# A block-sparse kernel whose expert numbers reach TensorE's registers in nine pieces instead of two loads

## Chip, cores and metric

One core of one Trainium2 chip runs the whole program. The metric is the device time of an execution in microseconds. TensorE (PE in the profile) multiplies matrices and has a stream for weight loads and register work of its own (PEld, PEldq); VectorE is DVE, ScalarE is ACT, GpSimd is POOL, SyncE is SP, which mostly issues DMAs.

## What is computed

Three parts run one behind the other in a single launch. A chunked linear attention over 4 x 8 x 768 x 32 values gives 3072 tokens of 256 channels. A first, dense "MoE" follows, and then a second one, with eight experts, of which each token takes the one with the largest gate:

```python
h = x @ w_in                       # 3072 x 256 -> 2048
x = (h * np.cos(h)) @ w_out        # 2048 -> 256
...
expert_idx = np.argmax(x @ w_gate, axis=1)
gate_w = probs[np.arange(N), expert_idx]
# each expert keeps its first `capacity` (768) tokens
h = np.maximum(np.einsum('ecd,edf->ecf', disp, w1), 0.0)   # 256 -> 1024
y = np.einsum('ecf,efd->ecd', h, w2)                       # 1024 -> 256
out[i] = gate_w[i] * y[expert_idx[i], pos[i]]
```

Which tokens go to which expert is known only when the kernel runs.

## The kernel before, in words

The tokens of the second MoE are sorted by expert into blocks of 128, each of one expert. There can be up to 31 blocks; 29 are always run, two more only behind a test at the end. The blocks come in two parts: 12 "early" blocks, from the tokens that have left the first MoE by then, and up to 19 "late" ones. Each part has a table, `eblk[0]` and `eblk[1]`, in which position n holds the expert number of its nth block. It is built by VectorE (L1141 to L1143).

A block's work is cut into two jobs, one for each half of the 1024 hidden channels; j counts the 58 jobs in order. The first 16 jobs are the first halves of blocks 0 to 15; the second halves of these come last. A job has these steps:

- `b_mm1` (L1603): six products of 128 x 512 into `hp`. The weights of the block's expert are picked by a register: `w[:, bass.ds(ev[i], 1), ...]`, so TensorE must hold block i's expert number in a register by then.
- `b_relu` (L1609, ScalarE) and `b_low` (L1613, VectorE) write the high and the low half-precision part of the result, `hr`.
- `b_turn`: for jobs 0 to 15 eight transposes on TensorE (L1630) that ScalarE copies to `ht` (L1639), for later jobs one transpose by DMA from SP's queue (L1634).
- `b_mm2` (L1650): twelve products of 128 x 256 into `yp`, with a register again. `b_out` (L1662 on ScalarE, L1664 on VectorE) scales and adds them, and `b_scat` (L1669, GpSimd) scatters a finished block.

`b_gather` and `b_xt` fetch a block's tokens (L1535) and transpose them by DMA (L1552). Beside the jobs run the units that prepare the second half's weights, `mk3` with `w2_units`: a pair of tiles `wst` is loaded from SP's queue (L1223, 512 KB a tile), ScalarE sums the squares of each (L1231), TensorE adds these over the partitions with two tiny products into `pn` (L1235), VectorE makes scales of that (L1240 to L1243), and the tiles are written as a high and a low part (L1250, L1252, L1256).

The registers are filled by `experts(k)`, once for each part of the blocks:

```python
regs = [nc.tensor.alloc_register(f"e{i}") for i in range(lo, hi)]
nc.tensor.reg_load(regs, eblk[k][0:1, 0:hi - lo])      # L1592
for i, r in zip(range(lo, hi), regs):
    ev[i] = nc.tensor.snap(r, min_val=0, max_val=E - 1)  # L1594
```

The load is one instruction on TensorE's sequencer (TENSOR_LOAD in the profile), and the register operations behind it show as FUSED_REGOPS. TensorE's loads, register operations and products are issued from one stream, in order.

The order of all this is written out by hand. The table `PLACE` gives every step a number; `put(name, fn, ...)` takes the next number of its name, and the steps are emitted by rising number, on all engines. `ex0` and `ex1` are the names under which `experts(0)` and `experts(1)` stand.

Of the kernel before, what the change touches and what calls it, by code (L numbers as in the profile page):

```python
# [95 lines left out]
    'con': [100],  # L96
    'cp': [188, 327, 352, 483, 628, 726, 836, 965, 1093, 1224],
    'css': [1523, 1570, 1609, 1639, 1670, 1687, 1709, 1747],
# [5 lines left out]
    'dfi': [206, 212, 232, 236, 345, 285, 302, 328],  # L104
    'et': [1404],
# [6 lines left out]
    'ex0': [1472],  # L112
    'ex1': [1658],
# [9 lines left out]
    'id': [1513],  # L123
    'in0': [1502],
    'in1': [1667],
    'iv0': [1499],
    'iv1': [1756, 1757, 1762],
    'lt': [1592],
    'lte': [1643],
    'lts': [1607],  # L130
    'ltt': [1623],
# [130 lines left out]
    'rev': [402, 403, 658, 661, 889, 895, 1113, 1123, 1328, 1329, 1517, 1520],  # L262
    'rex': [1245, 1405, 1576],
    'rg1': [565, 783, 1016, 1232, 1359, 1567],
    'rg2': [625, 846, 1083, 1295, 1421, 1578],
    'rh0': [479, 689, 957, 1192, 1370, 1535],
    'rh2': [502, 775, 984, 1280, 1385, 1557],
    'rl0': [497, 745, 967, 1195, 1384, 1545],
    'rl2': [648, 847, 1039, 1299, 1397, 1581],
# [11 lines left out]
    'rst': [662, 923, 1122, 1300, 1434, 1599],  # L281
    'rx0': [406, 675, 901, 1127, 1332, 1521],
    'rx1': [432, 670, 912, 1132, 1330, 1522],
    'rx2': [471, 712, 953, 1167, 1352, 1540],
    'rx3': [450, 706, 917, 1139, 1334, 1537],
# [20 lines left out]
    'uh': [1325, 1371, 1435, 1506],  # L306
    'ul': [1344, 1351, 1408, 1409, 1476, 1463, 1515, 1530],
    'un': [1287, 1360, 1411, 1461],
    'used': [1863],
# [25 lines left out]
def fused_kernel(ctx: ExitStack, tc: tile.TileContext, I, out: bass.AP):  # L335
    nc = tc.nc
# [42 lines left out]
    NE = 12  # L379
    LOS = ((0, NE), (NE, NB))  # L380
    gat = [base.tile([P, 20], I32, name=f"gat{k}") for k in range(2)]
    scat = [base.tile([P, 20], I32, name=f"scat{k}") for k in range(2)]
    eblk = [base.tile([P, 20], I32, name=f"eblk{k}") for k in range(2)]
# [894 lines left out]
    def put(name, fn, *a):  # L1278
        k = seen.get(name, 0)
        seen[name] = k + 1  # L1280
        work.append((PLACE[name][k], len(work), fn, a))
# [113 lines left out]
    for it in range(NIT):  # L1395
        t, f = divmod(it, NF)
# [192 lines left out]
    def experts(k):  # L1589
        lo, hi = LOS[k]  # L1590
        regs = [nc.tensor.alloc_register(f"e{i}") for i in range(lo, hi)]
        nc.tensor.reg_load(regs, eblk[k][0:1, 0:hi - lo])  # L1592
        for i, r in zip(range(lo, hi), regs):
            ev[i] = nc.tensor.snap(r, min_val=0, max_val=E - 1)  # L1594
# [105 lines left out]
    put('ete', t_expert, 0)  # L1700
    put('ett', t_token, 0)
    put('ex0', experts, 0)
    put('lt', late_tables)
    put('lts', t_sum, 1)
    put('lte', t_expert, 1)
    put('ltt', t_token, 1)
    put('ex1', experts, 1)
    put('iv0', b_iv, 0)
    put('in0', b_inv, 0, 0)
# [24 lines left out]
    used = []  # L1734
# [77 lines left out]
```

## Time and profile before

| | us |
|---|---|
| median of three executions (568.5 to 569.3) | 568.72 |
| the profiled execution, its own time | 568.56 |
| its span, first to last instruction | 566.8 |
| TensorE busy | 528.7 (93%) |
| VectorE busy | 415.7 (73%) |
| ScalarE busy | 379.2 (67%) |
| GpSimd busy | 355.6 (63%) |

The mean granted clock of TensorE over the span is 0.984. The shares are means over stages with different limits, so they say little of one place; the profiled execution's time and its span differ by what lies before the first and behind the last instruction.

### The profile page before, as it was taken

The page shows a single profiled execution, that of the slowest core. Times are in us where ns is not written, and L with a number is a line of the kernel's source. Part 1 is how long each engine was busy: PE and PEld are TensorE (multiplying, and loading weights), DVE is VectorE, ACT ScalarE, POOL GpSimd, SP SyncE. Part 2 cuts the span into 40 slices and gives each one's busy share as a digit, 9 for nine tenths or more (in the row PEclk, how much of TensorE's full clock was granted, in tenths as well). Part 3 has the DMA queues.
Part 4 walks back from the last instruction along what each step waited for, and adds up shares of the span by engine and source line. Part 5 has one row for each costly group of instructions (what it writes and reads, how often), then busy time and mean ns, then how long its engine had stood idle before and what let it go on. Part 6 is the DMA issues. An engine that isn't in the chain of part 4 may idle for free.

```text
span 566.8 us, 10500 instructions
## 1 busy us (share of the span) xinstructions
PE 528.7 (93%) x3188; PEld 387.9 (68%) x3188; DVE 415.7 (73%) x877; ACT 379.2 (67%) x691; POOL 355.6 (63%) x422
## 2 busy tenths in 40 slices
PE   8778999999999999999999998899589999998993
PEld 7455666877878778887888686665357666665672
DVE  6999985669977987688788999989957632332441
ACT  5448998887788688868887887788388633323210
POOL 5775374878668869876955673887546454312454
PEclk9999999999999999999999998999789999999998
DMA  6898533666264365263522331576587688767882
GB/s 227 276 318 323 191 116 128 186 246 220 94 222 132 99 201 177 82 201 116 166 58 76 85 102 38 144 185 174 139 198 204 113 160 162 157 118 131 152 164 63
DMA packets 110645, 89.91 MB, mean 159 GB/s; under 512 B 64542, under 2 KB 99424, under 8 KB 110592
## 3 DMA queue, kind: packets, MB, share of 16 engines
q1 hardware_dynamic: 107808, 82.26, 52.5%
q0 software_dynamic: 2784, 6.97, 4.8%
q8 instruction: 30, 0.49, 0.4%
q14 instruction: 23, 0.19, 0.1%
HBM read 59.50 MB, written 15.54 MB: 132 GB/s over the span
## 4 chain that ended last, share of the span: by engine, by line
PE 45%; DVE 25%; ACT 11%; DMA 7%; issue 6%; POOL 3%; SPq 1%; POOLq 0%; ACTq 0%; DVEq 0%
PE hp L1603 10%; PE hp L921 9%; PE yp L1650 9%; PE yt L959 7%; DVE g L938 4%; DVE g L932 3%; ACT g L935 3%; DMA out_dram<-yacc,scat 2%; PE yt L964 2%; ACT ex L646 2%; ACT g L928 2%; DVE w2a L1256 1%; DVE xs L1037 1%; POOL out_dram L1669 1%; ACT gh L942 1%
## 5 line engine op out<-in xcount | busy, mean ns | idle before, releaser
L921 PE MATMUL hp<-xT,w_in 128*128 128x512 f32 x576 | 153.7, 406 | 4.7 <-DVE g L938 2.5
L921 PEld LDWEIGHTS hp<-xT,w_in 128*128 128x128 f32 x576 | 104.9, 189 | 35.0 <-DVE g L938 8.8
L947 POOL TENSOR_TENSOR gw<-g,gh 128x512 fp32r<-128x512 f32 x72 | 98.8, 1376 | 47.6 <-ACT gh L942 22.8
L959 PE MATMUL yt<-gh,w_o 128*128 128x512 f32 x320 | 88.4, 398 | 0.1
L935 ACT ACTIVATE g<-g,halfpi 128x512 f32<-128x512 f32 x96 | 67.9, 717 | 27.0 <-DVE g L932 26.4
L1650 PEld LDWEIGHTS <-ht 128*128 128x128 f16 x696 | 68.0, 98 | 20.7 <-issue 2.7
L1609 ACT ACTIVATE hr<-hp 128x512 f16<-128x512 f32 x58 | 33.7, 596 | 72.2 <-PE hp L1603 43.1
L938 DVE TENSOR_TENSOR g<-hp,g 128x512 f32<-128x512 f32 x96 | 65.4, 685 | 18.0 <-ACT g L935 17.8
L932 DVE SCALAR_TENSOR_TENSOR g<-g,hp 128x512 f32<-128x512 f32 x96 | 64.4, 679 | 16.9 <-ACT g L928 16.2
L1613 DVE SCALAR_TENSOR_TENSOR hr<-hp,hr 128x512 f16<-128x512 f32 x58 | 39.2, 686 | 40.0 <-ACT hr L1609 35.6
L959 PEld LDWEIGHTS yt<-gh,w_o 128*128 128x128 f32 x320 | 58.3, 188 | 12.7 <-issue 1.0
L928 ACT ACTIVATE g<-hp 128x512 f32<-128x512 f32 x96 | 55.0, 586 | 17.9 <-PE hp L921 15.3
L942 ACT ACTIVATE gh<-g 128x512 fp32r<-128x512 f32 x80 | 48.7, 622 | 11.0 <-DVE g L938 6.5
L959 PE MATMUL yt<-gw,w_o 128*128 128x512 f32 x160 | 50.9, 399 | 1.6 <-POOL gw L947 0.8
L1535 POOL DMA_INDIRECT xr<-xs_d,gat x29 | 34.3, 1181 | 20.0 <-DMA xk<-xr 7.5
L1650 PE MATMUL yp<-w2b,ht 128*128 x348 | 43.2, 272 | 1.7 <-ACT yacc L1662 1.6
L1650 PE MATMUL yp<-w2a,ht 128*128 x348 | 44.2, 274 | 0.4 <-ACT ht L1639 0.4
L1669 POOL DMA_INDIRECT out_dram<-yacc,scat x29 | 28.9, 997 | 23.1 <-DVE yacc L1664 15.7
L629 POOL TENSOR_TENSOR ex<-ex,ncum 128x512 f32<-128x512 f32 x32 | 37.5, 1193 | 3.3 <-DMA ex<-cumc_d 2.1
L1657 POOL TENSOR_TENSOR sc<-gall,invb 128x1 f32<-128x1 f32 x58 | 12.7, 231 | 42.2 <-ACT yacc L1662 30.9
L1664 DVE SCALAR_TENSOR_TENSOR yacc<-yp,sc,yacc 128x256 f32<-128x256 f32 x29 | 13.5, 481 | 32.3 <-PE yp L1650 23.6
L959 PEld LDWEIGHTS yt<-gw,w_o 128*128 128x128 f32 x160 | 29.5, 189 | 11.1 <-POOL gw L947 3.3
(244 smaller groups left out, 995.3 us busy)
## 6 DMA issues: line engine op xcount, KB each, us to landing
wst<-in_w_dram SPq DMA_DIRECT2D x32, 512.0 KB
ex<-cumc_d SPq DMA_DIRECT2D x10, 1024.0 KB
pre<-in_w_io_dram SPq DMA_DIRECT2D x14, 512.0 KB
hl_d<-hl SPq DMA_DIRECT2D x10, 512.0 KB
b<-hl_d SPq DMA_DIRECT2D x10, 512.0 KB
c4s<-hl_d SPq DMA_DIRECT2D x40, 128.0 KB
xb<-in_xB_dram SPq DMA_DIRECT2D x11, 384.0 KB
xs_d<-xs SPq DMA_DIRECT2D x6, 514.0 KB
```

The source lines that it names most:

```text
L629: nc.gpsimd.tensor_tensor(lt, lt, nn, op=ALU.add)
L921: nc.tensor.matmul(hp, w_in[:, f, wl, k, :], xT[:, k, xl, :], start=(n == 0), stop=(n == 5))
L928: nc.scalar.activation(g, HP[it], AF.Copy, bias=MAGIC + 0.25)
L932: nc.vector.scalar_tensor_tensor(g, g, MAGIC, HP[it], op0=ALU.subtract, op1=ALU.subtract)
L935: nc.scalar.activation(GT[it], GT[it], AF.Sin, scale=SIN_SCALE, bias=halfpi)
L938: nc.vector.tensor_tensor(GT[it], HP.pop(it), GT[it], op=ALU.mult)
L942: nc.scalar.activation(h, GT[it], AF.Copy)
L947: eng.tensor_tensor(l, GT.pop(it), GH[it][0].bitcast(F32), op=ALU.subtract)
L959: nc.tensor.matmul(YT[t][k], WO['w'][:, f, o, k * P:(k + 1) * P], r, start=(f == 0 and n == 0), stop=(f == NF - 1 and n == 2))
L1603: nc.tensor.matmul(hp, XK[i][:, 2 * xl + k, :], w[:, bass.ds(ev[i], 1), k, wl, :].rearrange("p a b -> p (a b)"), start=(n == 0), stop=(n = ...
L1613: nc.vector.scalar_tensor_tensor(hr[:, 1], HPB.pop(j), 0.0, hr[:, 0], op0=ALU.max, op1=ALU.subtract)
L1650: nc.tensor.matmul(yp, ht[:, hk, :], w[:, bass.ds(e, 1), k, wl, :].rearrange("p a b -> p (a b)"), start=(k == 0 and n == 0), stop=(k == 3 ...
```

## The change

`ex0` and `ex1` are taken out. In their place stand nine steps, each of which loads the numbers of three to five blocks: blocks 0-2, 3-5, 6-8, 9-11 of the early part, and 12-14, 15-17, 18-21, 22-25, 26-30 of the late part. Each stands, by its number, behind the first products of some job, and ahead of the first job of its blocks. All other steps keep their order among each other; their numbers only make room, and so the diff of the table is cut to a few lines.

```diff
-    'ex0': [1472],
-    'ex1': [1658],
+    'e0': [1472],
+    'e12': [1672],
+    'e15': [1690],
+    'e18': [1760],
+    'e22': [1810],
+    'e26': [1876],
+    'e3': [1506],
+    'e6': [1552],
+    'e9': [1611],
...
-    def experts(k):
-        lo, hi = LOS[k]
-        regs = [nc.tensor.alloc_register(f"e{i}") for i in range(lo, hi)]
-        nc.tensor.reg_load(regs, eblk[k][0:1, 0:hi - lo])
-        for i, r in zip(range(lo, hi), regs):
+    def experts(k, a, b):
+        regs = [nc.tensor.alloc_register(f"e{i}") for i in range(a, b)]
+        nc.tensor.reg_load(regs, eblk[k][0:1, a - LOS[k][0]:b - LOS[k][0]])
+        for i, r in zip(range(a, b), regs):
             ev[i] = nc.tensor.snap(r, min_val=0, max_val=E - 1)
...
-    put('ex0', experts, 0)
+    for a, b in ((0, 3), (3, 6), (6, 9), (9, NE)):
+        put(f'e{a}', experts, 0, a, b)
...
-    put('ex1', experts, 1)
+    for a, b in ((12, 15), (15, 18), (18, 22), (22, 26), (26, LOS[1][1])):
+        put(f'e{a}', experts, 1, a, b)
```

Lines of these functions and behind them move down by six or seven: L1592 becomes L1598, L1594 becomes L1600, L1603 becomes L1609, L1650 becomes L1656, and L1235 becomes L1242.

On TensorE the second load stood between a job's last products and the next job's first ones. Before, at that place (`eblk_90` is the late part's table, ISA a register operation, `hp` and `yp` the results of first and second products):

```order
L1650 ISA
L1650 MATMUL yp_4562<-w2a,ht 128x256
L1603 LDWEIGHTS xkeep_4156 [waits DMAHW7_49]
L1592 TENSOR_LOAD eblk_90 [waits DVE_49]
L1594 ISA x2
L1603 ISA
L1603 MATMUL hp_4621<-w1a,xkeep_4156 128x512
L1603 LDWEIGHTS xkeep_4156
L1603 ISA
L1603 MATMUL hp_4621<-w1a,xkeep_4156 128x512
```

Of the change, at the same place:

```order
L1656 ISA
L1656 MATMUL yp_4565<-w2a,ht 128x256
L1609 LDWEIGHTS xkeep_4152 [waits DMAHW7_49]
L1609 ISA
L1609 MATMUL hp_4585<-w1a,xkeep_4152 128x512
L1609 LDWEIGHTS xkeep_4152
L1609 ISA
L1609 MATMUL hp_4585<-w1a,xkeep_4152 128x512
```

The load and its two register operations are gone there; the products that were around them now follow each other.

Two of the places where late pieces stand now, of the change. The second piece (blocks 15 to 17) lies between a job's first products and another's second ones:

```order
L1609 ISA
L1609 MATMUL hp_4712<-w1a,xkeep_4551 128x512
L1609 LDWEIGHTS xkeep_4551
L1609 ISA
L1609 MATMUL hp_4712<-w1a,xkeep_4551 128x512
L1656 LDWEIGHTS ht [waits Activation_49]
L1598 TENSOR_LOAD eblk_90
L1600 ISA
L1656 MATMUL yp_4742<-w2a,ht 128x256
L1656 LDWEIGHTS ht
L1656 ISA
L1656 MATMUL yp_4742<-w2a,ht 128x256
```

Before, the same products follow each other there without a load. The fourth piece (blocks 22 to 25) lies between two jobs' first products:

```order
L1609 LDWEIGHTS xk
L1609 ISA
L1609 MATMUL hp_5175<-w1b,xk 128x512
L1609 LDWEIGHTS xk [waits DMAHW3_49]
L1598 TENSOR_LOAD eblk_90
L1600 ISA
L1609 MATMUL hp_5194<-w1a,xk 128x512 [waits DVE_49]
```

There, too, nothing but the load and its register operation is new. The loads are the only instructions of TensorE that have moved.

## Rows read from the trace of the kernel before

**Rows 1.** Busy time by stretch of the kernel, the whole second MoE among them.

```profile
core 0: us, PE busy (x) PEld busy (x) DVE busy (x) ACT busy (x) POOL busy (x), PEclk, DMA share, GB/s
362.00:404.70 42.70, 33.84 (x222) 22.42 (x222) 39.80 (x98) 31.92 (x59) 29.88 (x40) 0.96 0.64 162
404.70:416.50 11.80, 11.74 (x86) 7.97 (x86) 9.40 (x22) 7.76 (x13) 8.94 (x12) 0.84 0.82 189
416.50:418.70 2.20, 0.04 (x1) 0.03 (x1) 2.17 (x4) 2.08 (x4) 0.00 (x0) 1.00 0.50 74
418.70:422.10 3.40, 3.40 (x15) 1.73 (x14) 0.63 (x2) 1.44 (x4) 1.38 (x3) 0.50 0.60 170
...
514.00:557.60 43.60, 43.58 (x306) 29.69 (x305) 17.62 (x33) 9.29 (x17) 21.09 (x36) 1.00 0.76 147
```

**Rows 2.** The chain of waits, 414 to 430 us: start, us, what.

```profile
...
416.46 2.21 issue
418.67 2.72 PE hp L1603 x6
421.38 0.85 PE tp L1630 x8
422.23 0.17 PE pn L1235 x2
...
423.73 1.29 PE hp L1603 x6
425.02 0.45 PE tp L1630 x8
...
428.08 0.12 PE pn L1235 x2
```

**Rows 3.** The register loads' line and their register operations: ns min/median/max, first and last start.

```profile
L1592 PEldq TENSOR_LOAD <-eblk x2: 1165/1507/1849, 365.8 to 416.1; - x2
...
L1594 PEldq FUSED_REGOPS  x4: 43/172/188, 367.1 to 418.3; - x4
```

**Rows 4.** TensorE's timeline at 367 and at 404 us: start, us, group.

```profile
367.47 1.20 PE L959 MATMUL yt<-gh,w_o 128*128 128x512 f32 x4
...
404.71 2.72 PE L1603 MATMUL hp<-w1a,xkeep 128*128 x6 [0.98 <-DVE hr L1613]
```

**Rows 5.** ScalarE's timeline, 415 to 428 us: the squares of the weight tiles.

```profile
...
418.99 0.19 ACT L1231 ACTIVATION_READ_ACCUMULATOR w2b<-wst 128x1 f32 x1
...
426.27 1.04 ACT L1231 ACTIVATE w2b<-wst 128x1024 f16<-128x1024 f32 x1
427.21 0.19 ACT L1231 ACTIVATION_READ_ACCUMULATOR w2b<-wst 128x1 f32 x1
```

**Rows 6.** The timeline of SP's queue, 404 to 435 us.

```profile
...
419.29 1.07 SPq L1223 DMA_DIRECT2D wst<-in_w_dram  x2
...
```

**Rows 7.** DMA traffic, 422.9 to 425.9 us, then 425.9 to 426.9.

```profile
DMA packets 1093, 0.70 MB, mean 232 GB/s; under 512 B 571, under 2 KB 1083, under 8 KB 1093
...
DMA packets 18, 0.01 MB, mean 14 GB/s; under 512 B 5, under 2 KB 18, under 8 KB 18
```

**Rows 8.** A job's register operations and products, 430 us and 462.9 us.

```profile
L1650 PEldq FUSED_REGOPS  x8: 51/55/55, 430.2 to 431.2; - x8
L1650 PE MATMUL yp<-w2a,ht x2: 272/272/273, 431.1 to 431.2; 128*128 x2
...
L1603 PEldq FUSED_REGOPS  x7: 51/55/55, 462.9 to 463.8; - x7
...
L1603 PE MATMUL hp<-w1a,xk x1: 379/379/379, 463.6 to 463.6; 128*128 x1
```

**Rows 9.** The loads of a single register, by queue of each engine.

```profile
...
L1736 PEldq TENSOR_LOAD <-eblk x1: 312/312/312, 475.3 to 475.3; - x1
...
L1736 SPq TENSOR_LOAD <-eblk x1: 1126/1126/1126, 475.9 to 475.9; - x1
...
```

**Rows 10.** TensorE's timeline, 510 to 516 us.

```profile
...
513.99 1.89 PE L1650 MATMUL yp<-w2b,ht 128*128 x12 [1.63 <-ACT yacc L1662]
```

More of the change, by code (lines that the diff above doesn't have):

```diff
@@ L94 @@
         1495, 1501, 1504],
[1 row of a table removed]
[1 row of a table added]
     'con': [100],
     'cp': [188, 327, 352, 483, 628, 726, 836, 965, 1093, 1224],
-    'css': [1523, 1570, 1609, 1639, 1670, 1687, 1709, 1747],
[1 row of a table removed]
+    'css': [1524, 1572, 1612, 1642, 1673, 1691, 1713, 1751],
[1 row of a table added]
     'df0': [121, 408, 546, 659, 760, 878, 969, 1141],
@@ L122 @@
     'gat': [148, 230, 350, 466, 585, 713, 838, 944, 1049, 1185],
-    'id': [1513],
+    'id': [1514],
     'in0': [1502],
-    'in1': [1667],
+    'in1': [1669],
     'iv0': [1499],
[L127 to L131, printed above, removed]
+    'iv1': [1761, 1762, 1767],
+    'lt': [1594],
+    'lte': [1646],
+    'lts': [1609],
+    'ltt': [1626],
     'm0': [193, 227, 316, 318, 363, 387, 517, 516, 605, 607, 756, 792, 880, 910, 1001, 986,
@@ L257 @@
     'raw': [65, 275, 353, 468, 599, 717, 822, 945, 1048],
[4 rows of a table removed]
[L262 to L269, printed above, removed]
[4 rows of a table added]
+    'rev': [402, 403, 658, 661, 889, 895, 1113, 1123, 1328, 1329, 1518, 1521],
+    'rex': [1245, 1405, 1578],
+    'rg1': [565, 783, 1016, 1232, 1359, 1569],
+    'rg2': [625, 846, 1083, 1295, 1421, 1580],
+    'rh0': [479, 689, 957, 1192, 1370, 1536],
+    'rh2': [502, 775, 984, 1280, 1385, 1559],
+    'rl0': [497, 745, 967, 1195, 1384, 1546],
+    'rl2': [648, 847, 1039, 1299, 1397, 1583],
     'rnd': [130, 137, 158, 181, 180, 197, 223, 242, 246, 278, 277, 315, 304, 319, 349, 351, 379,
@@ L276 @@
         1485],
[4 rows of a table removed]
[L281 to L285, printed above, removed]
[4 rows of a table added]
+    'rst': [662, 923, 1122, 1300, 1434, 1601],
+    'rx0': [406, 675, 901, 1127, 1332, 1522],
+    'rx1': [432, 670, 912, 1132, 1330, 1523],
+    'rx2': [471, 712, 953, 1167, 1352, 1541],
+    'rx3': [450, 706, 917, 1139, 1334, 1538],
     's0': [169, 218, 269, 306, 358, 382, 487, 480, 589, 606, 728, 786, 869, 893, 995, 974, 1107,
@@ L305 @@
     'ud': [1276, 1349, 1400, 1455],
-    'uh': [1325, 1371, 1435, 1506],
-    'ul': [1344, 1351, 1408, 1409, 1476, 1463, 1515, 1530],
+    'uh': [1325, 1371, 1435, 1507],
+    'ul': [1344, 1351, 1408, 1409, 1476, 1463, 1516, 1531],
     'un': [1287, 1360, 1411, 1461],
-    'used': [1863],
+    'used': [1869],
     'uss': [1312, 1369, 1429, 1486],
```

124 rows, old and new, of the table PLACE are left out of this document.

## The prediction

> **What bounds the kernel now.** I read the stretches first, then the chain of waits inside the one stretch where TensorE stands, then the rows of the two loads, then who feeds TensorE just behind them. By the table of stretches [rows 1] the kernel has two regimes around the change. From 362 to 404.7 us VectorE is busy 39.80 of 42.70 us and TensorE only 33.84: the end of the first MoE, which VectorE sets. From 404.7 on TensorE is busy almost all the time (11.74 of 11.80 us, then 43.58 of 43.60 in the last stretch): the second MoE, which TensorE sets, at full clock apart from its restarts. In it there is one hole, 416.5 to 418.7, and behind the hole a stretch at a granted clock of 0.50, the lower of TensorE's two levels, 1.2 GHz.
>
> The chain of waits tells the same in steps [rows 2]: an "issue" of 2.21 us at 416.46, in which TensorE waits for nothing but its own instruction stream, then six products of a job in 2.72 us and eight transposes in 0.85 us, where the same groups take 1.29 and 0.45 us a little later. The hole is the second load: the two loads of expert numbers took 1165 and 1849 ns [rows 3] for 12 and 19 registers, 97 ns a register in both, and the register operations that close them 172 ns each in the middle. A product of the second MoE can't be issued before the load ahead of it is done, since one stream feeds TensorE.
>
> **The first load (12 registers) becomes four loads.** Its register operations start at 367.1 us [rows 3] and TensorE's next group at 367.47 [rows 4], behind six products that were already issued, so at most 0.2 us was lost there, and in a stretch that VectorE sets [rows 1]. Three of the four pieces stay in that stretch. The fourth stands behind the first products of the second MoE, six in 2.72 us at half clock [rows 4], which cover its half microsecond. I take 0 for all four (ends: -0.2 and +0.3, one whole load of one register uncovered).
>
> **The second load leaves its place.** What it offers is the hole and the clock: 2.21 + (2.72 - 1.29) + (0.85 - 0.45) = 2.21 + 1.43 + 0.40 = 4.04 us. I count the clock in full, since it was at full level before the hole and at half behind it; with no hole there the fall has no occasion.
>
> **What takes it back: the weights of the second half.** Behind the job stand two tiny products (pn) that sum the squares of a pair of weight tiles. They wait for ScalarE, which squares the tiles.
> - First pair: ScalarE's last step starts at 418.99 and takes 0.19 us [rows 5], so the sum can't start before 419.18. Without hole and half clock TensorE is there at 416.46 + 1.29 + 0.45 = 418.20: a new wait of 0.98 us. Started at 419.2 instead of 422.23 [rows 2], the gain is 3.0 us.
> - Second pair: from the first sum to the second the chain needs 428.08 - 422.23 = 5.85 us [rows 2], so TensorE is there at 425.05. Its tiles were issued on SP's queue from 419.29 [rows 6], which the change does not touch; the DMA engines move 0.70 MB between 422.9 and 425.9 and then nearly nothing for a microsecond [rows 7]. So the second tile is in at about 425.9 whatever TensorE does. ScalarE squares it at 426.27 and is done at 427.21 + 0.19 = 427.40 [rows 5]; with its earlier work out of the way it can begin at 425.9, which gives 425.9 + 1.04 + 0.19 = 427.13. TensorE waits 2.1 us there, and the gain left is 428.08 - 427.13 = 0.95 at most; 428.08 - 427.40 = 0.68 if ScalarE isn't earlier.
>
> Behind this the products restart with nothing issued ahead, where before TensorE had work in hand; the restart lies between 0 and 0.3 us, with the 312 ns of the shortest register load on TensorE's stream [rows 9] as the nearest row for its starting anew. The later pairs of tiles, the transposes by DMA and the gathers then have to come earlier too for the rest of the gain to live to the end. They share queues and DMA engines that the change leaves as they are. I let half of it live: -0.4 us (ends -0.95, all of it, and +0.3, no gain and a late restart).
>
> **The five late pieces.** A piece costs TensorE only what its load exceeds the lead of the sequencer by. The lead is read where a job's stream begins. At the second late piece's place the job's first register operation is at 430.2 and its first product at 431.1: 0.9 us. At the fourth, ahead of one more job's first products, they are at 462.9 and 463.6: 0.7 us [rows 8]. The same two rows at the third and fifth place give 1.0 and 1.2 us and aren't shown. The price of a small load isn't in the trace of this line. From below: 97 ns a register as in the long loads [rows 3], 0.29 to 0.49 us. From above: TensorE's one load of a single register took 312 ns [rows 9], and 97 for each further one makes 0.51 to 0.70. With 0.17 for the register operation a piece is 0.46 to 0.87 us. Only the fourth can stick out: 0.31 + 0.29 + 0.17 - 0.7 = 0.07. The first late piece stands between the two waits above, and what it costs goes into the second. I take 0 (ends 0 and +0.1): the single register's row is the nearest, and even by it the leads cover.
>
> The Trainium skill speaks against cutting a load up: its page "DMA: Bandwidth & Descriptors", section "Latency and other measured facts", gives a register load from memory a floor of about 600 ns and says that the compiler groups loads to spread it. TensorE's row of 312 ns [rows 9] lies below that floor, so the trace disagrees for this engine. By the page's figure as the price of the first register, the pieces would stick out by about 0.5 us in all (an estimate), and the sum would be near +0.1 instead of -0.4.
>
> **Sum.** 0 - 4.04 + 3.1 (of it 0.98 at the first sum and 2.1 at the second) gives the 0.95; less the half that I let go, -0.4; pieces 0. The profiled execution took 568.56 us (span 566.8), 0.16 below the median of 568.72; -0.4 on either gives 568.2 and 568.3. A difference under 0.2%, 1.14 us, can hardly be told from none in a measurement of this kernel.
>
> **Rivals.**
> - *Full gain.* If the tiles land as much earlier as TensorE does, or the sums' wait is not on the path, the 4.0 us stay: 568.7 - 4.0 = 564.7. For it: each tile buffer comes free by work that TensorE's first sum releases, so later loads may start earlier. Against: the second pair's issue at 419.29 [rows 6] lies ahead of any of that. Chance 0.10. Between it and the forecast, with 1.2 to 2.5 us kept (around 567), 0.13.
> - *Slower by the loads.* If a load on TensorE has the price of SP's single register, 1126 ns [rows 9], instead of 312, the pieces cost 1.13 + 0.19 + 0.17 = 1.49, then 1.59, 1.59 and 1.69 for four and five registers, against leads of 0.9, 1.0, 0.7 and 1.2 us: 0.6 + 0.6 + 0.9 + 0.5 = 2.6 us stick out, less 0.4 is +2.2, 570.9. It decides from a first register of 0.57 us, where what sticks out is 0.4; it can be measured as slower from 0.87. For it: the price of one register runs from 312 to 1126 between two engines. Against: both long loads on TensorE show no fixed part at all, 97 ns a register at 12 and at 19. Chance 0.08.
> - *Slower by the clock.* The new wait of 2.1 us at the second sum is as long as the hole, and behind the hole the clock fell to half. If it falls there again, 1.83 us (1.43 + 0.40) are paid a second time: 568.3 + 1.8 = 570.1. Against: TensorE waited 1.63 us ahead of 513.99 too [rows 10], and the clock behind that is 1.00 [rows 1]. A fall decides the sign as soon as it comes, since 1.83 us stand against a gain of 0.4. Chance 0.09.
> - *The change doesn't do what it says.* By the order of instructions there are nine loads on TensorE, and no other engine's instructions change places. Chance 0.
>
> **The numbers.** The forecast, no measurable change around 568.3, has 0.60, and by its ends (-1.15 to +0.4 about the sum of terms) lies between 567.3 and 569.3. The range takes in the partial gain and half of the cases of a clock that falls: 566.7 to 570.1; out of it stay the full gain and most of the slower loads. Faster by over 0.2%: 0.10 + 0.13 and a little of the forecast's low end, 0.25. Slower by over 0.2%: 0.08 + 0.09, 0.17. The rest, 0.58, is no change.
>
> **What would show it.** Right: nine register loads of 0.3 to 0.6 us on TensorE's sequencer; no idle of 2.21 us at 416.5 and a clock of 1.00 right behind; TensorE waiting for ScalarE's squares about 1.0 us at the first sum and about 2 at the second; its last products ending near 557, as before. Wrong: no wait at the second sum, or tiles landing before 425.9 (then the full gain); idle time with "issue" at the later pieces (then the loads); a stretch at half clock after the second sum (then the clock).

## The result, and the profile after

The changed kernel takes 571.4 us (median of six, 570.7 to 571.8) against 569.01 us of before: 1.006 of it, with a 95% interval of 1.0037 to 1.0084. It is slower by 2.4 us, outside the forecast's range. The profiled execution took 571.78 us, its span is 570.1 (566.8 before).

The line of the loads, to compare with [rows 3]: its first row holds all nine loads (ns min/median/max, first and last start), the others each late piece by itself:

```profile
L1598 PEldq TENSOR_LOAD <-eblk x9: 768/1218/1923, 365.3 to 480.1; - x9
...
L1598 PEldq TENSOR_LOAD <-eblk x1: 782/782/782, 422.2 to 422.2; - x1
L1598 PEldq TENSOR_LOAD <-eblk x1: 969/969/969, 428.6 to 428.6; - x1
L1598 PEldq TENSOR_LOAD <-eblk x1: 1815/1815/1815, 444.7 to 444.7; - x1
L1598 PEldq TENSOR_LOAD <-eblk x1: 1714/1714/1714, 463.6 to 463.6; - x1
L1598 PEldq TENSOR_LOAD <-eblk x1: 1923/1923/1923, 480.1 to 480.1; - x1
```

The forecast had 0.46 to 0.87 us for a piece with its register operation. The late loads alone took 0.78, 0.97, 1.82, 1.71 and 1.92 us for 3, 3, 4, 4 and 5 numbers. Four registers at the third place took 0.85 us more than three at the second, while 19 registers together had taken 1.85 [rows 3].

TensorE's timeline after (start, us, group, in brackets the idle time before it and what ended it) shows the price:

```profile
416.80 1.46 PE L1609 MATMUL hp<-w1a,xkeep 128*128 x6
418.10 0.61 PE L1636 MATMUL tp<-ncum,hr 128*128 128x128 f16 x8
419.80 0.38 PE L1242 MATMUL pn<-wsc,ones_f 128*128 128x2 f32 x2 [1.09 <-ACT w2b L1238]
...
423.27 0.61 PE L1636 MATMUL tp<-ncum,hr 128*128 128x128 f16 x8 [0.30 <-issue]
...
426.32 0.28 PE L1242 MATMUL pn<-wsc,ones_f 128*128 128x2 f32 x2
...
429.81 1.77 PE L1656 MATMUL yp<-w2a,ht 128*128 x12 [0.16 <-ACT yacc L1668]
...
446.88 1.74 PE L1656 MATMUL yp<-w2a,ht 128*128 x12 [1.02 <-ACT w2b L1257]
...
465.62 1.46 PE L1609 MATMUL hp<-w1a,xk 128*128 x6 [1.35 <-issue]
...
482.33 1.81 PE L1656 MATMUL yp<-w2a,ht 128*128 x12 [0.82 <-issue]
...
517.45 1.92 PE L1656 MATMUL yp<-w2b,ht 128*128 x12 [1.67 <-ACT yacc L1668]
```

At 423.27, 429.81, 446.88, 465.62 and 482.33 TensorE stands behind each of the five late pieces: 0.30 + 0.16 + 1.02 + 1.35 + 0.82 = 3.65 us. The rows at 429.81 and 446.88 name ScalarE, but the load at the second lasts from 444.7 to 446.6, with a register operation of 0.17 behind it, and the first product follows 0.05 us later; at 429.81 it is the same, with a register operation that ends at 429.77. After three of these stops twelve second products take 1.74 to 1.81 us in place of the usual 1.47, some 0.3 us a time: the stream has nothing issued ahead there, and register operations and products then alternate, a pair in 0.13 us. The same groups in the timeline of before, to compare with:

```profile
421.18 1.05 PE L1630 MATMUL tp<-ncum,hr 128*128 128x128 f16 x8
422.03 0.37 PE L1235 MATMUL pn<-wsc,ones_f 128*128 128x2 f32 x2
...
427.91 0.28 PE L1235 MATMUL pn<-wsc,ones_f 128*128 128x2 f32 x2
...
446.68 1.47 PE L1650 MATMUL yp<-w2a,ht 128*128 x12
```

So the balance is: at the transposes behind the old hole the change is 3.1 us ahead (418.10 against 421.18), at the first sum 2.2 (419.80 against 422.03), at the second 1.6 (426.32 against 427.91). At the third piece it is 0.2 us late (446.88 against 446.68), at the fourth 2.0 (465.62 against 463.6 in [rows 8]), and at the wait of 517.45, which stood at 513.99 before [rows 10], 3.5. The spans differ by 3.3.

The stretches of [rows 1] at the old hole, after:

```profile
404.70:416.50 11.80, 11.80 (x84) 8.00 (x83) 8.42 (x21) 7.15 (x12) 8.74 (x12) 0.76 0.75 192
416.50:418.70 2.20, 2.20 (x19) 1.28 (x16) 2.20 (x3) 2.20 (x5) 0.93 (x2) 1.00 0.54 119
418.70:422.10 3.40, 2.31 (x18) 1.69 (x18) 2.27 (x8) 3.17 (x7) 2.18 (x4) 1.00 0.83 250
```

The hole and the half clock behind it are gone as forecast: 2.20 busy of 2.20, and a granted clock of 1.00 in both. The restart ahead of it stayed longer at half clock in this execution (0.76 in place of 0.84).

### The profile page after: what moved, and what is told of

Read it like the earlier page. It is cut to its first block, busy times and chain, and to the rows that moved or that the text cites. A ratio compares the mean times of both kernels' runs of the same rounds, so it can differ in the third digit from the quotient of the medians.

```text
span 570.1 us, 10507 instructions
## 1 busy us (share of the span) xinstructions
PE 529.1 (93%) x3188; PEld 386.8 (68%) x3188; DVE 415.6 (73%) x877; ACT 378.8 (66%) x691; POOL 357.3 (63%) x422
## 5 line engine op out<-in xcount | busy, mean ns | idle before, releaser
L1656 PEld LDWEIGHTS <-ht 128*128 128x128 f16 x696 | 68.2, 98 | 26.0 <-issue 7.2
L1656 PE MATMUL yp<-w2a,ht 128*128 x348 | 46.1, 277 | 3.3 <-issue 1.2
L1542 POOL DMA_INDIRECT xr<-xs_d,gat x29 | 35.6, 1227 | 16.1 <-DMA xk<-xr 5.5
L1656 PE MATMUL yp<-w2b,ht 128*128 x348 | 43.3, 272 | 1.7 <-ACT yacc L1668 1.7
```

Source lines behind the costliest of these rows:

```text
L1542: nc.gpsimd.indirect_dma_start(out=xr, out_offset=None, in_=xs_d, in_offset=bass.IndirectOffsetOnAxis(ap=gat[k][:, n:n + 1].bitcast(U32), ...
L1656: nc.tensor.matmul(yp, ht[:, hk, :], w[:, bass.ds(e, 1), k, wl, :].rearrange("p a b -> p (a b)"), start=(k == 0 and n == 0), stop=(k == 3 ...
```

## Where the loss is: the late pieces

**One part of the change at a time.** In late_only the early part is loaded at once:

```diff
-    for a, b in ((0, 3), (3, 6), (6, 9), (9, NE)):
+    for a, b in ((0, NE),):
```

> The early part's 12 numbers in one load again, the late part in five pieces as in the change. Theory A (the price of the late pieces: the trace after shows 0.78 to 1.92 us a piece, and TensorE standing at each): all of the loss is here, 571.4 us, +2.4 over before. Theory B (my forecast's chain: weights and DMA transposes set the end, pieces cost nothing): 568.5 to 569. Theory C (the early pieces hold up the clock after 404 us, 0.84 us lost there): 570.5, 0.9 less than the change.

Measured: 573.85 us against 570.04 of before on the same chip, ratio 1.0068 (1.0040 to 1.0096). In early_only the late part is loaded at once, in its old place:

```diff
-    'e12': [1672],
+    'e12': [1660],
...
-    for a, b in ((12, 15), (15, 18), (18, 22), (22, 26), (26, LOS[1][1])):
+    for a, b in (LOS[1],):
```

> The early part in four pieces as in the change, the late part's 19 numbers in one load at its old place. Theory A: 569.0, no difference to before, since the early pieces lie in a stretch that VectorE sets. Theory B: the same 569.0. Theory C: 569.8 to 570, and the half clock behind 404 us lasts some 2 us longer than in before.

Measured: 571.24 us, ratio 1.0009 (0.9979 to 1.0038). The late pieces alone bring the whole loss, so theory A holds. Theory C would have left late_only at 1.003, below its interval. A small share of the early pieces can't be excluded by early_only.

**One load, moved.** one_before_sum keeps the two loads of before and moves the second, and so does one_behind_job:

```diff
-    'ex1': [1658],
+    'ex1': [1661.5],
```

> The two loads of before, the second one moved behind a job's first products and the transposes, just ahead of the sums over partitions at which TensorE has to wait for ScalarE's squares anyway. Theory A: the load of 1.85 us lies beside that wait of 1.0 us and the lead of the sequencer; TensorE has no hole at 416.5 and no half clock behind, and no pieces are paid: 567 us, 2 less than before. Theory B: the gain is taken back by the weights and the transposes all the same: 568.5 to 569.

Measured: 568.61 us, ratio 0.9974 (0.9946 to 1.0002). In one_behind_job the number is 1669.5.

> The two loads of before, the second one moved to the place of the change's first late piece, behind the first products of the next job. Theory A: 1.85 us stand against a lead of about 0.5 us, so some 1.3 us of idle time there; with 2.2 to 3 us gained ahead of it the end is near 568, 1 less than before. Theory B: the load fills a wait that TensorE has at the next sums anyway: 568.5 to 569, as one_before_sum.

Measured: 569.76 us, ratio 0.9996 (0.9975 to 1.0018). Neither is clear of before. Both are clear of the change, so it is not a new place for the load that costs, it is the cut.

## What makes a short load dear

The next two kernels add loads of numbers that TensorE already holds, by a step that loads any range of a table again:

```diff
+    def again(k, a, b):
+        regs = [nc.tensor.alloc_register(f"x{len(NX)}_{i}") for i in range(a, b)]
+        nc.tensor.reg_load(regs, eblk[k][0:1, a - LOS[k][0]:b - LOS[k][0]])
...
```

price_swap changes the counts at the places of the late pieces two to five (the single second load is at the first).

> Single second load at the first late piece's place, and loads of numbers already held at the places of the other four late pieces, with other counts: 19 registers at the second place (the change: 3 in 0.97 us), 12 at the third (4 in 1.82), one at the fourth (4 in 1.71), three at the fifth (5 in 1.92). If the place sets the price (what else moves at that time), the times stay near 1 (plus 16 registers), 1.8, 1.7 and 1.9 us. If the count sets it, 12 registers take about 1.2 us, one 0.3 and three 0.8, whatever the place.

The four loads, in order of place:

```profile
L1708 PEldq TENSOR_LOAD <-eblk x1: 1832/1832/1832, 430.2 to 430.2; - x1
L1708 PEldq TENSOR_LOAD <-eblk x1: 4570/4570/4570, 447.4 to 447.4; - x1
L1708 PEldq TENSOR_LOAD <-eblk x1: 302/302/302, 471.3 to 471.3; - x1
L1708 PEldq TENSOR_LOAD <-eblk x1: 1354/1354/1354, 487.0 to 487.0; - x1
```

The single register is quick where four had taken 1.71 us, and 19 took no longer at the second place than at 416: the place alone does not set the price. Neither does the count: twelve registers took 4.57 us at the third place, and TensorE stood for it:

```profile
452.55 2.72 PE L1651 MATMUL yp<-w2a,ht 128*128 x12 [4.00 <-issue]
```

These twelve begin at position 3 of the table, the twelve that took 1165 ns before [rows 3] at position 0. One execution took 577.15 us, against 569.87 of before.

price_tail adds loads late in the kernel. Its edit puts twelve; nine are in the trace, and by their order these are the nine of the expectation.

> The kernel before with nine more loads of numbers already held, behind jobs' first products from about 485 us to the end, of 4, 19, 5, 3, 4, 12, 3, 3 and 19 registers; the seventh and eighth are back to back. If a load has a fixed price of about 0.7 us and 97 ns a register, they take 1.1, 2.5, 1.2, 1.0, 1.1, 1.9, 1.0, 1.0 and 2.5 us. If 3 registers are cheap and 4 and more dear by themselves: 1.7 to 1.9 for 4 and 5, 0.8 for 3. If the place sets the price, equal counts differ by as much as 1 us.

Five of the nine, of 4, 19, 5, 4 and 12 registers from positions 0, 0, 3, 8 and 0:

```profile
L1708 PEldq TENSOR_LOAD <-eblk x1: 625/625/625, 499.4 to 499.4; - x1
L1708 PEldq TENSOR_LOAD <-eblk x1: 2974/2974/2974, 503.7 to 503.7; - x1
L1708 PEldq TENSOR_LOAD <-eblk x1: 1492/1492/1492, 511.1 to 511.1; - x1
L1708 PEldq TENSOR_LOAD <-eblk x1: 870/870/870, 529.3 to 529.3; - x1
L1708 PEldq TENSOR_LOAD <-eblk x1: 1242/1242/1242, 533.8 to 533.8; - x1
```

None of the expectation's three explanations accounts for the whole list: 4 registers took 0.63 and 0.87 us here and 1.7 to 1.8 in the change, where they began at positions 6 and 10; five from position 3 took 1.49. The 19 (2.97 us) were slower than at any other place. One execution took 579.83 us. A new theory came of it, theory D in the next runs: a load that begins at a multiple of four of the table's positions fetches its registers in groups of four, another one by one. Theory E is that the place sets the price.

**The same cut in other places of the table.** recut leaves the five places and moves the borders:

```diff
-    for a, b in ((12, 15), (15, 18), (18, 22), (22, 26), (26, LOS[1][1])):
-        put(f'e{a}', experts, 1, a, b)
+    for p, a, b in ((12, 12, 16), (15, 16, 20), (18, 20, 24), (22, 24, 28), (26, 28, LOS[1][1])):
+        put(f'e{p}', experts, 1, a, b)
```

> The change with the late part cut at multiples of four: blocks 12-15, 16-19, 20-23, 24-27, 28-30 at the same five places. In the runs so far loads that begin at a table position that is a multiple of four and hold four or more cost 97 to 220 ns a register (4 in 0.63 and 0.87 us, 12 in 1.2, 19 in 1.8), all others 257 to 450 (12 from position 3 in 4.57 us). Theory D (a load is quick where it begins at a multiple of four, else each register is fetched by itself): the first four pieces take 0.6 to 0.9 us, the last, of three, 0.8 to 1.4; TensorE's loss at the last three places falls from 3.7 us to under 1, and the end is near 568.5, some 3 less than the change. Theory E (the place sets the price): pieces of 0.8 to 1.9 us as in the change, 571.4.

```profile
L1598 PEldq TENSOR_LOAD <-eblk x1: 343/343/343, 420.9 to 420.9; - x1
L1598 PEldq TENSOR_LOAD <-eblk x1: 342/342/342, 426.7 to 426.7; - x1
L1598 PEldq TENSOR_LOAD <-eblk x1: 329/329/329, 442.3 to 442.3; - x1
L1598 PEldq TENSOR_LOAD <-eblk x1: 335/335/335, 460.0 to 460.0; - x1
L1598 PEldq TENSOR_LOAD <-eblk x1: 1381/1381/1381, 475.6 to 475.6; - x1
```

Four registers took 329 to 343 ns from positions 0, 4, 8 and 12, less than theory D gave them; the left-over three took 1.38 us. Measured: 567.83 us against 567.72, ratio 1.0012 (0.9992 to 1.0031). The loss is gone. In offsets4 nine loads follow each other behind one job's first products, from positions 0 to 8, so that neither place nor count differs:

```diff
+    for x in [(0, 0, 4), (0, 1, 5), (0, 2, 6), (0, 3, 7), (0, 4, 8), (0, 5, 9), (0, 6, 10), (0, 7, 11), (0, 8, 12)]:
+        put('dm', again, *x)
```

> The kernel before with nine loads of four numbers back to back, behind one job's first products, from table positions 0, 1, 2 ... 8. Theory D: those from 0, 4 and 8 take about 0.6 us, the others 1.0 to 1.8, in one and the same place. Theory E: nine times about the same.

The loads from 0, 1, 2, 3 and 4, and the last, from 8:

```profile
L1708 PEldq TENSOR_LOAD <-eblk x1: 338/338/338, 495.8 to 495.8; - x1
L1708 PEldq TENSOR_LOAD <-eblk x1: 1984/1984/1984, 496.3 to 496.3; - x1
L1708 PEldq TENSOR_LOAD <-eblk x1: 1006/1006/1006, 498.5 to 498.5; - x1
L1708 PEldq TENSOR_LOAD <-eblk x1: 1445/1445/1445, 499.7 to 499.7; - x1
L1708 PEldq TENSOR_LOAD <-eblk x1: 370/370/370, 501.3 to 501.3; - x1
...
L1708 PEldq TENSOR_LOAD <-eblk x1: 339/339/339, 506.2 to 506.2; - x1
```

From 0, 4 and 8 it is 0.34 to 0.37 us, from the other six 1.0 to 1.98. offsets8 does the same with eight registers:

> The same with five loads of eight numbers from positions 0, 1, 2, 3, 4. Theory D: from 0 and 4 about 1 us, from 1, 2 and 3 two to three. Theory E: about the same for all five.

From 0, 1 and 4 (2 and 3 took 2.89 and 2.52):

```profile
L1708 PEldq TENSOR_LOAD <-eblk x1: 597/597/597, 498.1 to 498.1; - x1
L1708 PEldq TENSOR_LOAD <-eblk x1: 2994/2994/2994, 498.9 to 498.9; - x1
...
L1708 PEldq TENSOR_LOAD <-eblk x1: 591/591/591, 507.9 to 507.9; - x1
```

Theory D foretold which loads are quick, and E did not. One execution of each took 573.73 and 577.13 us.

**Fewer than four are dear as well.** recut_pad is recut with the last piece read as four registers, the fourth of them unused:

```diff
-        regs = [nc.tensor.alloc_register(f"e{i}") for i in range(a, b)]
-        nc.tensor.reg_load(regs, eblk[k][0:1, a - LOS[k][0]:b - LOS[k][0]])
+        regs = [nc.tensor.alloc_register(f"e{i}") for i in range(a, b + (b == NB))]
+        nc.tensor.reg_load(regs, eblk[k][0:1, a - LOS[k][0]:a - LOS[k][0] + len(regs)])
```

> As recut, with the last piece of three numbers read as four, from position 16 (the fourth is the count of blocks, which nothing uses here). Theory D: that load falls from 1.4 us to 0.35, and TensorE loses 0.4 us less than in recut; of the end not more than that. If three registers were slow for another reason than being fewer than four, it stays above 1 us.

```profile
L1598 PEldq TENSOR_LOAD <-eblk x1: 333/333/333, 478.3 to 478.3; - x1
```

A register more, and 0.33 us in place of 1.38. So the runs show what a load costs by its first position and its count; that the hardware fetches the others one by one is the reading that fits them, and no run shows it by itself. Measured: 567.56 us, ratio 0.9988 (0.9967 to 1.0009). one_pad_sum reads 20 registers in one load in the place of one_before_sum, with the same edit in its `experts`.

> As one_before_sum, with the second load read as 20 numbers instead of 19, so that nothing is left over beyond the groups of four. Theory D: a register more, and yet shorter than the 1.8 to 2.3 us of 19: some 1.4 us (five groups of 0.27 each, as eight registers took 0.59). The end near one_before_sum's, 0.3% below before, at most half a microsecond better. If each register costs the same: 1.95 to 2.2 us.

```profile
L1592 PEldq TENSOR_LOAD <-eblk x1: 1611/1611/1611, 416.2 to 416.2; - x1
```

20 took 1.61 us, 19 in the same place 2.11: shorter, though not quite the 1.4 expected. Measured: 567.14 us against 567.71, ratio 0.9996 (0.9971 to 1.0021); the gain over before that was expected did not show.

## What is left of the gain when the loads are cheap

recut_sum takes recut, the early part in one load, and the first late piece ahead of the sums:

```diff
-    'e12': [1672],
+    'e12': [1663.5],
...
-    for a, b in ((0, 3), (3, 6), (6, 9), (9, NE)):
+    for a, b in ((0, NE),):
```

> As recut, with the early part's 12 numbers in one load again, and the first late piece just ahead of the sums at which TensorE waits for ScalarE. Theory D: the first piece is hidden by that wait, the next three by the leads of 0.7 to 1.0 us but for 0.3 in all: 567 us, 2 less than before. Theory E: about 571.

Measured: 567.5 us against 567.72, ratio 1.0005 (0.9979 to 1.0032): the 2 us did not come. The change and recut were then run on one chip.

> The changed kernel itself, on one chip with the next three. Theory D: 0.6% over before, as it was; the last three late pieces take 1.7 to 1.9 us again, 4 and 5 registers from positions 6, 10 and 14.

> The late part cut at multiples of four, a second time. Theory D: 2 to 4 us below the change on the same chip. Open is how it stands to before: by my forecast's chain (the squares and the transposes take the gain back) within 0.2% of it; by the profile of the first time, in which TensorE is 2.3 us ahead of before from the last piece to the end, 0.4% faster.

Measured: the change 571.84 us, ratio 1.0066 (1.0037 to 1.0094); recut 567.99 us, ratio 1.0000 (0.9983 to 1.0017); before 567.71. The cut at multiples of four is worth 3.9 us, and with it the kernel stands where it stood before the change. The first profile of recut (565.94 us) was the lowest of its twelve executions; in it TensorE is 2.3 us ahead of before at the last piece, and only 1.6 ahead from there to its last products, not 2.3 to the end as the expectation says. The profile of recut_again (571.25) is the highest of its twelve. So neither is typical. In recut_again TensorE's timeline at the two sums reads:

```profile
420.42 0.38 PE L1242 MATMUL pn<-wsc,ones_f 128*128 128x2 f32 x2 [1.01 <-ACT w2b L1238]
...
428.34 0.38 PE L1242 MATMUL pn<-wsc,ones_f 128*128 128x2 f32 x2 [1.67 <-ACT w2b L1238]
```

These are the waits that the forecast had put at 0.98 and 2.1 us: 1.01 and 1.67, for ScalarE's squares. In the profile of change_again the second is longer still:

```profile
418.96 0.38 PE L1242 MATMUL pn<-wsc,ones_f 128*128 128x2 f32 x2 [0.74 <-ACT w2b L1238]
...
428.01 0.38 PE L1242 MATMUL pn<-wsc,ones_f 128*128 128x2 f32 x2 [2.00 <-ACT w2b L1238]
428.26 2.21 PE L1609 MATMUL hp<-w1a,xkeep 128*128 x6
```

SP issued that pair of tiles at 419.24, as before at 419.29 [rows 6], and ScalarE's second square began only when its tile was there:

```profile
419.24 1.07 SPq L1230 DMA_DIRECT2D wst<-in_w_dram  x2
```

```profile
426.81 1.06 ACT L1238 ACTIVATE w2b<-wst 128x1024 f16<-128x1024 f32 x1 [0.27 <-DMA wst<-in_w_dram]
```

Behind this wait of 2.00 us TensorE ran at half clock again, which was a rival of its own in the prediction (the stretch behind the wait, with the columns of [rows 1]):

```profile
428.30:431.50 3.20, 3.20 (x16) 1.71 (x17) 2.27 (x5) 1.69 (x4) 2.34 (x3) 0.58 1.55 239
```

The six products at 428.26 took 2.21 us instead of 1.46. Behind the wait of 1.67 in recut_again they took 1.46, so the clock doesn't fall each time. In the change's first profile the tiles were issued 1.2 us earlier, and TensorE did not wait at the second sum at all. The pair stands on SP's queue behind transposes of tokens; SP issued it at 416.60 in the first profile of recut and at 420.51 in recut_again.

The profile of recut_pad is nearest to what the forecast supposed: all five late loads are cheap (0.33 to 0.45 us), and its 567.83 us are close to the median of 567.56.

```profile
419.71 0.38 PE L1242 MATMUL pn<-wsc,ones_f 128*128 128x2 f32 x2 [1.23 <-ACT w2b L1238]
...
426.98 0.38 PE L1242 MATMUL pn<-wsc,ones_f 128*128 128x2 f32 x2 [0.91 <-ACT w2b L1238]
```

TensorE is 2.3 us ahead of before at the first sum (419.71 against 422.03) and 0.9 at the second (426.98 against 427.91). At the fourth piece's products it is 0.5 ahead (463.10 against 463.62), and at the wait of 513.99 0.5 late (514.54). So how much of the gain lives differs from execution to execution; over all of them recut keeps nothing that can be measured.

## Why the prediction was wrong

- **The old hole** (4.04 us on offer): right. The hole is gone and the clock behind it full, in every profile without a load there.
- **The first sum's wait** (0.98 us): right, 1.09 after, 0.74 to 1.66 in the runs above.
- **The second sum's wait** (2.1 us): right as a mechanism, but not as a fixed size. It was 2.00 in change_again, 1.67 in recut_again, 0.91 in recut_pad, 0.49 in recut_sum, and none in the first profiles of the change and of recut. It hangs on when the tiles land, which I took as fixed. One of the prediction's signs of being wrong, no wait at the second sum, showed in the change's first profile; the full gain did not follow, since the late pieces took more than it.
- **The early pieces** (0): nothing measured against it; early_only's interval leaves room for a small share.
- **The late pieces** (0, ends 0 and +0.1): the step that failed. They came to 3.65 us of idle time, and some 0.3 us at each of three restarts. The leads were right: with 0.9, 1.0, 0.7 and 1.2 us, the loads of 0.97, 1.82, 1.71 and 1.92 us and 0.14 to 0.18 us of register operation stick out by 0.2, 1.0, 1.2 and 0.9; measured were 0.16, 1.02, 1.35 and 0.82. The price was wrong. I took both ends from loads of whole tables and of one register, and both rows were of favourable kinds: the long loads begin at position 0, and a single register pays for one fetch. Neither bounds four registers from position 6.
- **The rival "slower by the loads"** had 2.6 us sticking out and 570.9, with a chance of 0.08; it came to 571.4. So it was near by its number, and not by its reason: a fixed price of 1.13 us is not what the runs show, since aligned groups of four cost 0.33. I argued it down with the 97 ns a register of the long loads, which say nothing of a load that begins elsewhere.
- **The rival "slower by the clock"** came in change_again's profile, and not in the change's first one, so the loss doesn't need it.
- **The rest of the sum**: with cheap loads, no measurable change is what recut, recut_sum and recut_pad gave (ratios 1.0012, 1.0005 and 0.9988). That the size fits is in part luck, since the second sum's wait differs so much between executions. The upper ends of the sum, 0.3, 0.3 and 0.1, add to +0.7 and not to +0.4; the failed step doesn't hang on it.
- **The Trainium skill's** "DMA: Bandwidth & Descriptors", section "Latency and other measured facts", had spoken against the cut with a floor of about 600 ns. The sign was right. The figure was not: loads of one and of four registers took 0.30 and 0.33 us, and those of the change 0.77 to 1.92.

Two things stay open. Why a register outside a group of four took some 260 ns in some places (768 / 3) and 450 to 550 in others (1815 / 4, 1639 / 3) was not settled. DMA traffic alone does not order them: three registers took 779 ns at 542.9 us in price_tail, with the DMA engines idle, and 768 at 405.2 us in the change, with a DMA share of 0.84. That it has a part can't be excluded, since three more took 1639 ns right behind the 779, with a share of 1.04. And it is open whether any version here beats before: one_before_sum with 0.9974 has an interval that still holds 1.

## What to carry to other kernels

Before a load of registers is cut into pieces, look at where each piece begins and ends, and not only at its size: the mean per element of a long, aligned one is no price for a short one. Here the whole loss came of the borders 15, 18, 22 and 26; with borders at multiples of four it is gone. And a hole removed ahead of an engine that is fed by transfers is worth only what the next landing allows: here a removed hole of 4 us left nothing that could be measured.

## What was not expected of the hardware

- Register loads on TensorE's stream, over all profiles: four registers from a multiple of four took 0.33 to 0.37 us in 18 of 22 loads (0.45, 0.60, 0.63 and 0.87 in the others), eight 0.59. From other positions four took 1.0 to 2.0 and eight 2.5 to 3.0. Twelve took 1.17 to 1.36 us from position 0 and 4.57 from position 3.
- Three registers cost 0.76 us at the least, and 0.78 at the least from position 0: more than twice the price of four.
